# Three of twelve normed tiles transposed by DMA instead of TensorE, their norm weights applied by ScalarE, and a normed-x tile for each batch

## The chip, the core and the metric

The kernel runs on one core of one Trainium2 chip. The metric is the device time of one execution in microseconds (us); less is better. Engines are named as in the profile: PE is TensorE's matmul, PEld its weight load, DVE is VectorE, ACT is ScalarE, POOL is GpSimd, and SP is SyncE, which here only issues DMAs. A trailing q (SPq) means an engine's sequencer.

## What is computed

An attention of the RWKV kind with a decaying state over 4 batches, 8 heads, 768 steps and head size 48, and on its output, as 3072 tokens of width 384, a root-mean-square norm and a gated feed-forward layer of width 1536:

```python
for t in range(S):
    cur = np.einsum('bhd,bhe->bhde', u[None] * kt, vt)
    y[:, :, t] = np.einsum('bhd,bhde->bhe', rt, state + cur)
    state = wt[:, :, :, None] * state + np.einsum('bhd,bhe->bhde', kt, vt)
...
xn = x / np.sqrt(np.mean(x * x, axis=-1, keepdims=True) + 1e-06) * rms_g
g = xn @ w_gate
out = (g / (1 + np.exp(-g)) * (xn @ w_val)) @ w_out
```

Inputs and output are float32. Matmuls run in bf16.

## The kernel before, in words

The sequence is cut into 6 superblocks `n` of 128 steps. A superblock holds 4 batches `j` of 128 tokens each, so 512 tokens. Every piece of work is a step with a name and two numbers, `step.n.j` (or `step.n.f`, where `f` is one of 12 slices of 128 units of the feed-forward layer). One long string, `ORDER`, lists all steps; a loop at the end calls the function of each in turn, and each function issues its instructions at once. So `ORDER` alone sets the order of instructions within each engine, and each engine works in that order; between engines, semaphores make a reader wait for its writer.

For one superblock: `load_*` fetch r, k, v, w (SP). `ln`, `cs_mm`, `cs_add`, `exp_r`, `exp_k`, `r_mul`, `k_mul` make the decayed r and k (ACT, PE, DVE, POOL); `w_tot` makes the state's decay (DVE). `rk_tr` transposes r and k, from superblock 2 on by a DMA that SP issues. `q_mm`, `q_mask_*`, `st_mm`, `st_new`, `y_mm`, `x_add` give the attention's output `xb`, 128 tokens by 384. Then the norm: `x_sq` (ACT) squares and sums, `x_rstd` (POOL) gives the factor, `xn_mul` (ACT) writes the normed `xn` in bf16. The feed-forward layer needs `xn` transposed, with the norm's weights `gT` applied, in the tile `xnt` of 128 x 3 x 512. This is done in two ways:

- superblocks 0 to 3: `xn_pe` makes three 128x128 transposes on PE into PSUM, and `xn_out` (DVE) copies them to `xnt` times `gT`, one instruction of 384 columns;
- superblocks 4 and 5: `xn_tr` transposes by one DMA from SP straight into `xnt`, and `xn_gain` multiplies all 512 tokens by `gT` in place, three instructions a superblock (DVE, one of them ACT).

`gate_mm` and `val_mm` (three matmuls of 512 columns each, line 626) read the whole of `xnt`; `silu` (ACT) and `h_mul` (DVE) give `ht`; `o_mm` (12 matmuls of 384 columns a batch, line 672) and `o_out`, `out_dma` bring the result out. The feed-forward layer of superblock n runs beside the attention of superblock n+1, and `o_mm` of n-1 fills PE between them: while it runs, the transposes for superblock n are made.

PSUM is used in three rings: "a" and "b" with 2 slots each (names `ps_au`, `ps_av`, `ps_bu`, `ps_bv`), taken in turn by `cs_mm`, `cs_add`, `gate_mm` and `val_mm`, and "q" with 4 slots (`ps_qu` and so on) for the rest, the transposes included. A slot goes to the step that asks when its last user is the oldest. `xn` has 3 buffers, taken in `xn_mul`; the squares that `x_sq` has no use for go to one fixed tile, `junk`.

Of the kernel before, what the change touches and what calls it, by code (L numbers as in the profile page):

```python
# [74 lines left out]
exp_k.3.3 cs_mm.3.2 xn_out.2.3 o_mm.1.2 load_r.3.2 k_mul.3.1 w_tot.3.3 rk_tr.3.0 r_mul.3.3 cs_add.3.2 out_dma.1.0
xn_out.2.1 load_v.3.0 exp_r.3.2 gate_mm.2.5 exp_k.3.2 r_mul.3.2 w_tot.3.2 val_mm.2.0 gate_mm.2.0 bonus_mul.3.0
bonus_mul.3.2 k_mul.3.2 o_out.1.3 bonus_sum.3.0 silu.2.5 rk_tr.3.1 load_k.3.3 o_out.1.2 q_mm.3.0 silu.2.0 q_mask_e.3.0
val_mm.2.1 bonus_v.3.0 h_mul.2.0 gate_mm.2.1 load_w.4.1 load_v.3.1 load_k.4.3 st_mm.3.2 k_mul.3.3 q_copy_o.3.0
silu.2.1 rk_tr.3.2 load_v.4.0 rk_tr.3.3 val_mm.2.5 gate_mm.2.11 load_k.4.0 bonus_sum.3.1 cast_v.3.0 out_dma.1.1
load_v.3.3 load_w.5.2 q_mask_e.3.1 q_copy_o.3.1 gate_mm.2.2 silu.2.11 h_mul.2.5 val_mm.2.2 h_mul.2.1 load_w.4.0  # L80
gate_mm.2.3 load_v.4.1 silu.2.2 q_mask_o.3.0 cast_v.3.1 load_r.4.1 bonus_sum.3.2 h_mul.2.2 bonus_v.3.1 gate_mm.2.6
val_mm.2.3 y_mm.3.0 st_new.3.2 st_mm.3.0 silu.2.3 gate_mm.2.4 h_mul.2.3 silu.2.6 q_mask_o.3.1 st_new.3.0 st_mm.3.1
silu.2.4 x_add.3.0 load_k.4.1 gate_mm.2.7 val_mm.2.4 x_sq.3.0 gate_mm.2.10 out_dma.1.2 cast_v.4.0 st_new.3.1
val_mm.2.6 q_mm.3.2 h_mul.2.4 bonus_mul.3.3 h_mul.2.6 silu.2.7 val_mm.2.7 val_mm.2.10 load_w.4.3 x_rstd.3.0 silu.2.10
# [5 lines left out]
o_out.2.0 x_rstd.3.2 xn_mul.3.2 w_tot.4.0 ln.4.2 exp_r.4.1 load_r.5.1 x_rstd.3.3 k_mul.4.0 xn_out.3.0 load_r.4.3  # L90
out_dma.1.3 bonus_sum.4.1 xn_pe.3.1 xn_out.3.1 ln.4.3 exp_k.4.1 bonus_mul.4.2 xn_mul.3.3 r_mul.4.1 k_mul.4.1 w_tot.4.1
out_dma.2.0 o_mm.2.1 cs_mm.4.2 xn_pe.3.3 bonus_mul.4.0 cast_v.4.1 xn_pe.3.2 o_out.2.1 cs_mm.4.3 bonus_sum.4.2
rk_tr.4.0 xn_out.3.3 cs_add.4.3 load_k.5.3 o_mm.2.3 exp_r.4.3 xn_out.3.2 cs_add.4.2 bonus_mul.4.3 r_mul.4.3 w_tot.4.3
exp_k.4.3 exp_r.4.2 rk_tr.4.1 o_out.2.3 exp_k.4.2 load_v.4.2 val_mm.3.1 gate_mm.3.6 bonus_sum.4.0 k_mul.4.3 r_mul.4.2
st_mm.4.0 w_tot.4.2 load_r.5.3 load_k.5.0 val_mm.3.0 o_out.2.2 silu.3.6 st_new.4.0 k_mul.4.2 gate_mm.3.1 q_mm.4.0
cast_v.4.2 out_dma.2.2 bonus_sum.4.3 silu.3.1 gate_mm.3.0 q_copy_o.4.0 silu.3.0 h_mul.3.1 q_copy_o.4.1 gate_mm.3.3
val_mm.3.6 gate_mm.3.8 rk_tr.4.3 q_mask_e.4.0 h_mul.3.0 h_mul.3.6 st_mm.4.1 bonus_v.4.0 q_mask_e.4.1 q_mask_o.4.0
load_r.5.0 bonus_v.4.2 rk_tr.4.2 load_v.5.1 q_mask_o.4.1 bonus_v.4.1 silu.3.3 gate_mm.3.4 val_mm.3.4 val_mm.3.3
y_mm.4.0 silu.3.4 st_new.4.1 gate_mm.3.9 h_mul.3.4 load_v.4.3 load_r.5.2 load_k.5.1 silu.3.8 x_add.4.0 val_mm.3.8
gate_mm.3.2 q_mm.4.2 h_mul.3.3 h_mul.3.8 silu.3.9 val_mm.3.9 load_w.5.1 silu.3.2 gate_mm.3.10 q_mask_e.4.3  # L100
q_copy_o.4.3 y_mm.4.1 h_mul.3.9 bonus_mul.5.3 x_sq.4.0 q_mask_o.4.3 x_rstd.4.0 q_copy_o.4.2 bonus_v.4.3 silu.3.10
x_add.4.1 load_w.5.3 val_mm.3.10 gate_mm.3.7 q_mask_e.4.2 x_sq.4.1 bonus_sum.5.3 xn_mul.4.0 load_w.5.0 x_rstd.4.1
h_mul.3.10 silu.3.7 val_mm.3.2 gate_mm.3.5 h_mul.3.2 load_k.5.2 gate_mm.3.11 q_mask_o.4.2 y_mm.4.2 cast_v.4.3
xn_mul.4.1 val_mm.3.7 silu.3.5 bonus_mul.5.0 x_add.4.2 silu.3.11 ln.5.1 y_mm.4.3 h_mul.3.7 val_mm.3.11 x_add.4.3
load_v.5.3 x_sq.4.2 xn_tr.4.0 h_mul.3.11 x_sq.4.3 xn_tr.4.1 val_mm.3.5 st_mm.4.3 h_mul.3.5 x_rstd.4.2 cs_mm.5.1
cs_add.5.1 ln.5.2 xn_mul.4.2 x_rstd.4.3 o_mm.3.2 o_out.3.2 cs_mm.5.2 xn_tr.4.2 exp_k.5.1 cs_add.5.2 exp_r.5.1 o_mm.3.0
xn_mul.4.3 r_mul.5.1 ln.5.3 ln.5.0 xn_tr.4.3 cs_mm.5.0 st_new.4.3 exp_r.5.2 cast_v.5.3 exp_k.5.2 o_mm.3.1 out_dma.3.2
cs_add.5.0 out_dma.2.3 r_mul.5.2 exp_r.5.0 cs_mm.5.3 r_mul.5.0 st_mm.4.2 exp_k.5.0 cs_add.5.3 exp_r.5.3 o_mm.3.3
bonus_mul.5.1 xn_gain.4.0 xn_gain.4.2 xn_gain.4.1 k_mul.5.0 r_mul.5.3 exp_k.5.3 o_out.3.1 out_dma.2.1 o_out.3.0
# [5 lines left out]
h_mul.4.4 bonus_sum.5.2 q_mm.5.2 q_copy_o.5.2 gate_mm.4.10 val_mm.4.6 bonus_v.5.3 cast_v.5.2 silu.4.8 h_mul.4.5
q_copy_o.5.3 cast_v.5.1 q_mask_e.5.3 q_mask_e.5.2 q_mask_o.5.2 silu.4.10 h_mul.4.6 gate_mm.4.7 x_sq.5.0 y_mm.5.1
q_mask_o.5.3 silu.4.7 bonus_v.5.2 x_rstd.5.0 x_add.5.1 val_mm.4.10 y_mm.5.3 val_mm.4.7 y_mm.5.2 gate_mm.4.11 x_add.5.3
x_sq.5.1 h_mul.4.10 x_sq.5.3 x_rstd.5.1 h_mul.4.7 xn_mul.5.1 val_mm.4.8 out_dma.3.3 gate_mm.4.9 silu.4.11 x_rstd.5.3
xn_mul.5.3 xn_tr.5.1 h_mul.4.8 xn_mul.5.0 val_mm.4.11 xn_tr.5.3 x_add.5.2 x_sq.5.2 x_rstd.5.2 val_mm.4.9 silu.4.9
# [5 lines left out]
val_mm.5.9 gate_mm.5.10 silu.5.9 h_mul.5.6 h_mul.5.9 val_mm.5.8 silu.5.10 val_mm.5.10 gate_mm.5.11 h_mul.5.8
h_mul.5.10 val_mm.5.11 silu.5.11 h_mul.5.11 o_mm.5.0 o_mm.5.3 o_out.5.3 o_mm.5.1 out_dma.5.3 o_out.5.1 o_out.5.0
out_dma.5.0 o_mm.5.2 out_dma.5.1 o_mm.5.4 o_out.5.2 out_dma.5.2 o_out.5.4 out_dma.5.4
# [597 lines left out]
```

## Time and profile before

| | |
|---|---|
| median of 3 runs | 201.12 us (200.55 to 201.53) |
| the profiled execution | 200.28 us, of which the span from first to last instruction is 198.6 us |
| TensorE clock granted | 1.000 of full speed |
| busy share of the span | PE 97%, DVE 76%, ACT 69%, POOL 63% |

The profile is of one execution. Rows of the timeline give start, duration, engine, line, operation, output<-input and, in brackets, the engine's idle time ahead of the row and what ended it; a row with xN joins N like instructions, from the first's start to the last's end. Matmul durations include the time through the pipeline, so the next one starts well before the one before has ended.

### The profile page before, as it was taken

To read this page: it belongs to the slowest core of one execution; us is meant where nothing else is said; L and a number is where in the kernel's file an instruction comes from. 1 tells how busy PE (TensorE), PEld (TensorE's weight loads), DVE (VectorE), ACT (ScalarE), POOL (GpSimd) and SP (SyncE) were. 2 spreads that over 40 slices of the span, in tenths; PEclk is the share of its full clock that TensorE was granted. 3 is DMA by queue.
4 is the path that set the end of the run, shared out by engine and by line. 5 is a ranking of instruction groups with operands and counts; after the bars stand their busy time and mean duration, and the time that the engine had idled before them with its cause. 6 is when DMAs were issued, how large, how long until landed. Compare 5 with 4: busy or idle time off the path is not lost.

```text
span 198.6 us, 4409 instructions
## 1 busy us (share of the span) xinstructions
PE 191.9 (97%) x1577; PEld 113.9 (57%) x1577; DVE 151.4 (76%) x290; ACT 137.3 (69%) x279; POOL 125.2 (63%) x184
## 2 busy tenths in 40 slices
PE   7979998999999999999999999999999999999994
PEld 3556574465665565665556665556655565555562
DVE  6358989989998799987889989987887973173611
ACT  4399989579979569958559959399786683164300
POOL 5378993189399687899939899867686851000000
PEclk9999999999999999999999999999999999999999
DMA  6999999999999998999899879995499012032012
GB/s 153 268 235 176 183 220 203 214 180 211 179 195 224 206 196 196 236 198 207 193 195 225 188 171 204 204 183 107 138 187 208 0 25 60 6 112 83 0 59 101
DMA packets 121566, 32.41 MB, mean 163 GB/s; under 512 B 116420, under 2 KB 120392, under 8 KB 121544
## 3 DMA queue, kind: packets, MB, share of 16 engines
q1 hardware_dynamic: 119504, 28.58, 67.3%
q0 software_dynamic: 2032, 3.54, 10.0%
q8 instruction: 12, 0.20, 0.4%
q14 instruction: 10, 0.08, 0.1%
q10 hardware_dynamic: 8, 0.00, 0.0%
HBM read 25.96 MB, written 4.72 MB: 154 GB/s over the span
## 4 chain that ended last, share of the span: by engine, by line
PE 72%; SPq 18%; DMA 6%; POOL 2%; issue 1%; ACT 0%; POOLq 0%
SPq L248 16%; PE ps_av L626 10%; PE ps_bu L626 10%; PE ps_bv L626 10%; PE ps_au L626 10%; PE ps_qv L672 7%; PE ps_qz L672 7%; PE ps_qu L672 5%; PE ps_qx L672 4%; DMA wo_sb<-in_moe_w_out_dram 4%; DMA vt<-in_v_dram 3%; SPq L261 2%; PE ps_qz L502 1%; PE ps_qx L552 1%; PE ps_av L417 1%
## 5 line engine op out<-in xcount | busy, mean ns | idle before, releaser
L672 PEld LDWEIGHTS <-ht 128*128 128x128 bf16 x300 | 28.2, 98 | 17.0 <-issue 0.5
L626 PEld LDWEIGHTS <-wg_sb 128*128 128x128 bf16 x216 | 23.1, 114 | 19.7 <-DMA wg_sb<-in_moe_w_gate_dram 0.7
L626 PEld LDWEIGHTS <-wv_sb 128*128 128x128 bf16 x216 | 22.8, 114 | 19.0 <-DMA wv_sb<-in_moe_w_val_dram 1.0
L658 DVE TENSOR_TENSOR ht<-ps_bv,sg 128x512 bf16<-128x512 f32 x35 | 24.0, 686 | 10.1 <-PE ps_bv L626 9.2
L235 ACT ACTIVATE sg<-ps_av 128x512 bf16<-128x512 f32 x37 | 22.0, 595 | 12.3 <-PE ps_av L626 12.0
L626 PE MATMUL ps_av<-xnt,wg_sb 128*128 128x512 bf16 x111 | 30.1, 380 | 0.0
L626 PE MATMUL ps_bu<-xnt,wv_sb 128*128 128x512 bf16 x111 | 30.1, 380 | 0.0
L658 DVE TENSOR_TENSOR ht<-ps_bu,sg 128x512 bf16<-128x512 f32 x37 | 25.4, 686 | 6.0 <-PE ps_bu L626 5.2
L626 PE MATMUL ps_bv<-xnt,wv_sb 128*128 128x512 bf16 x105 | 28.5, 380 | 0.6 <-DMA wv_sb<-in_moe_w_val_dram 0.5
L626 PE MATMUL ps_au<-xnt,wg_sb 128*128 128x512 bf16 x105 | 28.5, 380 | 0.2 <-DMA wg_sb<-in_moe_w_gate_dram 0.2
L235 ACT ACTIVATE sg<-ps_au 128x512 bf16<-128x512 f32 x35 | 21.0, 599 | 10.8 <-PE ps_au L626 9.0
L467 POOL TENSOR_TENSOR ruk<-rt,kt 128x384 f32<-128x384 f32 x24 | 24.1, 1003 | 6.6 <-DMA kt<-in_k_dram 4.8
L468 POOL TENSOR_TENSOR ruk<-ruk,u_bc 128x384 f32<-128x384 f32 x24 | 24.4, 1017 | 1.9
L520 POOL TENSOR_SCALAR_AFFINE_SELECT qts<-qts 128x512 bf16<-128x512 bf16 x20 | 12.9, 653 | 15.1 <-ACT qts L513 14.6
L477 POOL TENSOR_TENSOR ydiag<-vt,diag 128x384 f32<-128x384 f32 x24 | 19.9, 833 | 1.0 <-DVE rk L461 0.5
L461 POOL TENSOR_TENSOR rk<-kt,ek 128x384 bf16<-128x384 f32 x16 | 15.9, 1007 | 2.3 <-ACT ek L235 2.3
L672 PE MATMUL ps_qv<-wo_sb,ht 128*128 128x384 bf16 (+1 forms) x96 | 15.0, 306 | 0.0
L672 PE MATMUL ps_qz<-wo_sb,ht 128*128 128x384 bf16 x84 | 14.8, 326 | 0.0
L233 ACT ACT_TABLE_LOAD x10 | 12.8, 1283 | 1.8 <-PEq L709 1.6
L235 ACT ACTIVATE lw<-wt 128x384 bf16<-128x384 f32 (+1 forms) x20 | 11.1, 578 | 4.2 <-DMA wt<-in_w_dram 4.1
L472 DVE TENSOR_REDUCE diag<-ruk 128x8 f32<-128x384 f32 x24 | 12.9, 543 | 0.7 <-POOL ruk L468 0.7
L585 ACT ACTIVATE xn<-xb,rstd 128x384 bf16<-128x384 f32 x20 | 11.8, 605 | 0.8 <-POOL rstd L580 0.8
(180 smaller groups left out, 373.6 us busy)
## 6 DMA issues: line engine op xcount, KB each, us to landing
rt<-in_r_dram SPq DMA_DIRECT2D x24, 192.0 KB, 3.9
kt<-in_k_dram SPq DMA_DIRECT2D x24, 192.0 KB, 4.0
vt<-in_v_dram SPq DMA_DIRECT2D x24, 192.0 KB, 3.7
out_dram<-ob SPq DMA_DIRECT2D x23, 192.0 KB, 2.3
wt<-in_w_dram SPq DMA_DIRECT2D x16, 192.0 KB, 4.0
wt<-in_w_dram SPq DMA_DIRECT2D x4, 384.0 KB, 4.4
wo_sb<-in_moe_w_out_dram POOLq DMA_DIRECT2D x3, 384.0 KB, 7.1
wg_sb<-in_moe_w_gate_dram POOLq DMA_DIRECT2D x1, 768.0 KB, 9.8
```

What stands on the lines that cost most here:

```text
L233: nc.scalar.preload_act_table_set(table_name)
L235: return nc.scalar.activation(**kw).ins
L248: dmas["load_" + which, n, j] = nc.sync.dma_start(out=inp[which, n, j], in_=t[j, :, n * L:(n + 1) * L, :].rearrange("h t d -> t h d")).ins
L461: eng.tensor_tensor(out=rk[:, n % 2, j, 1, :, 0:D], in0=inp["k", n, j], in1=bank["cs_k", n, j][:, 0:DM].rearrange("p (h d) -> p h d", h=H) ...
L467: nc.gpsimd.tensor_tensor(out=ruk[n, j], in0=inp["r", n, j], in1=inp["k", n, j], op=ALU.mult)
L468: nc.gpsimd.tensor_tensor(out=ruk[n, j], in0=ruk[n, j], in1=u_bc, op=ALU.mult)
L472: nc.vector.tensor_reduce(out=diag[n, j].rearrange("p h o -> p (h o)"), in_=ruk[n, j], axis=mybir.AxisListType.X, op=ALU.add)
L477: nc.gpsimd.tensor_tensor(out=ydiag[n, j], in0=inp["v", n, j], in1=diag[n, j].to_broadcast([128, H, D]), op=ALU.mult)
L520: nc.gpsimd.affine_select(out=qts[n, j][:, 1], in_=qts[n, j][:, 1], compare_op=ALU.is_gt, fill=0.0, base=0, pattern=[[0, NP], [1, 128]], c ...
L626: nc.tensor.matmul(ps[:, cols], lhsT=units(ws, c, f), rhs=xnt[n][:, c, cols], start=(first and c == 0), stop=(c == KC - 1))
L658: nc.vector.tensor_tensor(out=ht[n][:, f, :], in0=bank.pop(("v", n, f)), in1=bank.pop(("sg", n, f)), op=ALU.mult)
L672: nc.tensor.matmul(ps[:, cols], lhsT=ht[n][:, f, b * L:(b + 1) * L], rhs=wo_sb[:, f, cols], start=(f == 0), stop=(f == FC - 1))
```

## The change

`ORDER` loses `xn_pe.2.0`, `xn_pe.3.0` and `xn_pe.3.1` and gains `xn_tr.2.0`, `xn_tr.3.0` and `xn_tr.3.1`. For these three, `xn_out` no longer reads PSUM by DVE but multiplies `xnt` in place by ACT, 128 columns in each of three instructions. `xn_out.2.0` moves two steps on, `xn_out.3.0` and `xn_out.3.1` some steps on, and `load_r.3.2` comes earlier, ahead of `xn_tr.2.0`. `xn` now has a buffer for each batch (4), is taken in `x_sq`, and takes the squares too, so that `junk` goes. All else in `ORDER` keeps its sequence; the table is cut here to one line.

```diff
-o_mm.1.3 w_tot.3.1 xn_pe.2.3 o_out.1.1 cs_add.3.3 r_mul.3.1 load_k.3.2 load_r.3.3 xn_pe.2.1 xn_out.2.0 exp_r.3.3
+xn_pe.2.3 o_out.1.1 cs_add.3.3 r_mul.3.1 load_k.3.2 load_r.3.3 load_r.3.2 xn_tr.2.0 xn_pe.2.1 exp_r.3.3 exp_k.3.3
...
     EARLY = 13
+    XT_DMA = sel("30 20 31")
...
-    junk = const.tile([128, DM], BF16)
...
-        nc.scalar.activation(out=junk, in_=xb[n, j], func=AF.Square, accum_out=rstd[n, j][:, 0, c:c + 1])
+        xn = bank["xn", n, j] = pt.tile([128, DM], BF16, name="xn", bufs=SB)
+        nc.scalar.activation(out=xn, in_=xb[n, j], func=AF.Square, accum_out=rstd[n, j][:, 0, c:c + 1])
...
     def xn_mul(n, j):
-        xn = bank["xn", n, j] = pt.tile([128, DM], BF16, name="xn", bufs=3)
+        xn = bank["xn", n, j]
...
             xnt[n] = pt.tile([128, KC, TS], BF16, name="xnt")
+        if (n, j) in XT_DMA:
+            for c in range(KC):
+                t = xnt[n][:, c, j * L:(j + 1) * L]
+                nc.scalar.activation(out=t, in_=t, func=AF.Copy, scale=gT[:, c:c + 1])
+            return
         ps = bank.pop(("xt", n, j))
```

How the instructions stand on SP at the turn to the feed-forward layer of superblock 3. Before (the `rt` are `load_r.4.0` and `load_r.4.2`, then `load_w.4.2`, `load_k.4.2`, `load_r.5.1`, `load_r.4.3`; the `rkT` is `rk_tr.4.0`):

```order
L261 DMA wt<-in_w_dram 128x8x48
L248 DMA rt<-in_r_dram 128x8x48 x2
L261 DMA wt<-in_w_dram 128x8x48
L248 DMA kt<-in_k_dram 128x8x48
L248 DMA rt<-in_r_dram 128x8x48 x2
L687 DMA out_dram<-ob 128x384 x2
L489 DMA_TRANSPOSE rkT<-rk 128x8x128
```

After (lines have moved on by one to six):

```order
L262 DMA wt<-in_w_dram 128x8x48
L249 DMA rt<-in_r_dram 128x8x48
L591 DMA_TRANSPOSE xnt<-xn 128x3x128
L249 DMA rt<-in_r_dram 128x8x48
L262 DMA wt<-in_w_dram 128x8x48
L249 DMA kt<-in_k_dram 128x8x48
L249 DMA rt<-in_r_dram 128x8x48 x2
L693 DMA out_dram<-ob 128x384
L591 DMA_TRANSPOSE xnt<-xn 128x3x128
L693 DMA out_dram<-ob 128x384
L489 DMA_TRANSPOSE rkT<-rk 128x8x128
```

`xn_tr.3.0` has come between the two `rt` loads, so that five loads and an output now stand behind it, and `xn_tr.3.1` between the two outputs.

ACT at the same place, before, from `exp_k.4.1` and `xn_mul.3.3` (line 585) over `o_out.2.1` (681) to `o_out.2.3`:

```order
L235 ACTIVATE ek<-ps_bu 128x384
L585 ACTIVATE xn<-xb,rstd 128x384
L681 COPY ob<-ps_qv 128x384
L235 ACTIVATE ps_av<-ps_av 128x388
L235 ACTIVATE ek<-ps_bv 128x384
L235 ACTIVATE ps_au<-ps_au 128x388
L681 COPY ob<-ps_qv 128x384
```

After:

```order
L236 ACTIVATE ek<-ps_bu 128x384
L586 ACTIVATE xn<-xb,rstd 128x384
L605 ACTIVATE xnt<-xnt,gT 128x128 x3
L687 COPY ob<-ps_qv 128x384
L605 ACTIVATE xnt<-xnt,gT 128x128 x3
L236 ACTIVATE ps_av<-ps_av 128x388
L236 ACTIVATE ek<-ps_bv 128x384
L236 ACTIVATE ps_au<-ps_au 128x388
L687 COPY ob<-ps_qv 128x384
```

The two times three new instructions stand on either side of `o_out.2.1`, both ahead of `exp_r.4.3` (`ps_av`) and `exp_k.4.3` (`ek<-ps_bv`). For superblock 2 the three of `xn_out.2.0` stand between `exp_k.3.3` and `exp_r.3.2`, and `xn_tr.2.0` stands on SP straight ahead of `rk_tr.3.0`.

More of the change, by code (lines that the diff above doesn't have):

```diff
@@ L75 @@
[L75 to L84, printed above, removed]
@@ L90 @@
[L90 to L99, printed above, removed]
@@ L100 @@
[L100 to L109, printed above, removed]
@@ L115 @@
[L115 to L119, printed above, removed]
@@ L125 @@
[L125 to L127 removed]
+load_r.3.0 x_sq.2.2 xn_mul.2.0 cast_v.3.2 cs_add.3.0 x_add.2.3 exp_k.3.0 x_sq.2.3 o_mm.1.0 cs_mm.3.1 exp_r.3.0 ln.3.2
+x_rstd.2.2 o_mm.1.1 st_new.2.3 load_r.3.1 out_dma.0.3 w_tot.3.0 r_mul.3.0 xn_mul.2.1 k_mul.3.0 xn_mul.2.2 cs_add.3.1
@@ new lines @@
+exp_k.3.1 xn_pe.2.2 cs_mm.3.3 x_rstd.2.3 o_out.1.0 exp_r.3.1 bonus_mul.3.1 xn_out.2.2 xn_mul.2.3 o_mm.1.3 w_tot.3.1
+xn_pe.2.3 o_out.1.1 cs_add.3.3 r_mul.3.1 load_k.3.2 load_r.3.3 load_r.3.2 xn_tr.2.0 xn_pe.2.1 exp_r.3.3 exp_k.3.3
+xn_out.2.0 cs_mm.3.2 xn_out.2.3 o_mm.1.2 k_mul.3.1 w_tot.3.3 rk_tr.3.0 r_mul.3.3 cs_add.3.2 out_dma.1.0 xn_out.2.1
+load_v.3.0 exp_r.3.2 gate_mm.2.5 exp_k.3.2 r_mul.3.2 w_tot.3.2 val_mm.2.0 gate_mm.2.0 bonus_mul.3.0 bonus_mul.3.2
+k_mul.3.2 o_out.1.3 bonus_sum.3.0 silu.2.5 rk_tr.3.1 load_k.3.3 o_out.1.2 q_mm.3.0 silu.2.0 q_mask_e.3.0 val_mm.2.1
@@ new lines @@
+x_add.3.3 cs_mm.4.0 bonus_mul.4.1 ln.4.1 cs_mm.4.1 x_sq.3.1 x_add.3.2 x_sq.3.2 cs_add.4.0 h_mul.2.8 st_new.3.3
+o_mm.2.0 x_sq.3.3 o_mm.2.2 exp_r.4.0 load_k.4.2 cs_add.4.1 exp_k.4.0 r_mul.4.0 x_rstd.3.1 xn_mul.3.1 o_out.2.0
+x_rstd.3.2 xn_mul.3.2 w_tot.4.0 ln.4.2 exp_r.4.1 load_r.5.1 x_rstd.3.3 k_mul.4.0 load_r.4.3 out_dma.1.3 xn_tr.3.1
+bonus_sum.4.1 ln.4.3 exp_k.4.1 bonus_mul.4.2 xn_mul.3.3 xn_out.3.0 r_mul.4.1 k_mul.4.1 w_tot.4.1 out_dma.2.0 o_mm.2.1
+cs_mm.4.2 xn_pe.3.3 bonus_mul.4.0 cast_v.4.1 xn_pe.3.2 o_out.2.1 xn_out.3.1 cs_mm.4.3 bonus_sum.4.2 rk_tr.4.0
```

61 lines of the change are left out of this document (44 added, 17 removed).

## The prediction

> **What bounds the kernel now.** I read the page's busy shares first, then the chain that ended last, then the timelines of PE, ACT and SP at the two turns where the three transposes stand.
>
> ```profile
> PE 191.9 (97%) x1577; PEld 113.9 (57%) x1577; DVE 151.4 (76%) x290; ACT 137.3 (69%) x279; POOL 125.2 (63%) x184
> DMA  6999999999999998999899879995499012032012
> PE 72%; SPq 18%; DMA 6%; POOL 2%; issue 1%; ACT 0%; POOLq 0%
> 46.00 7.12 DMA wo_sb<-in_moe_w_out_dram
> 53.16 0.81 PE ps_qx L672 x4
> ...
> 194.63 1.00 PE ps_qv L672 x12
> ```
>
> The chain leaves the loads at 53.16 us and is PE's from there to the end. All that the change moves lies behind that point, in a stretch where PE never waits long: an instruction less on PE is time gained, and a helper's lateness costs only what it makes PE wait. The DMA row matters too: the 16 engines are nearly full until about 130 us, and all three new DMAs fall into that time.
>
> **Off PE: nine transposes.** Three groups go, `xn_pe.2.0`, `xn_pe.3.0` and `xn_pe.3.1`:
>
> ```profile
> 82.66 0.33 PE L596 MATMUL ps_qx<-ident,xn 128*128 128x128 bf16 x3
> 82.83 2.11 PE L672 MATMUL ps_qu<-wo_sb,ht 128*128 128x384 bf16 x12
> 109.32 0.33 PE L596 MATMUL ps_qx<-ident,xn 128*128 128x128 bf16 x3
> 109.48 2.11 PE L672 MATMUL ps_qv<-wo_sb,ht 128*128 128x384 bf16 x12
> 113.38 0.33 PE L596 MATMUL ps_qu<-ident,xn 128*128 128x128 bf16 x3
> 113.55 2.11 PE L672 MATMUL ps_qv<-wo_sb,ht 128*128 128x384 bf16 x12
> ```
>
> A group is shown as 0.33 us, but the next starts 0.17, 0.16 and 0.17 us after it: that is what it takes of PE. The sum is -0.50 us. Nothing else on PE changes but the names of PSUM slots, which I cost at nothing: three users fewer of the "q" ring leave each slot free for longer.
>
> **Off DVE: three copies** of 0.55 us (the last `xn_out` of superblock 2, below, is of that form). DVE is not on the chain, so this is worth nothing by itself.
>
> **Onto ACT: nine instructions of 128 columns.** No row has this size in place. The nearest are one in-place multiply of 512 columns and `xn_mul`, 384 columns:
>
> ```profile
> L612 ACT ACTIVATE xnt<-xnt,gT x1: 712/712/712, 145.0 to 145.0; 128x512 bf16<-128x512 bf16 x1
> L585 ACT ACTIVATE xn<-xb,rstd x20: 597/600/618, 51.5 to 165.4; 128x384 bf16<-128x384 f32 x20
> 111.50 1.10 ACT L585 ACTIVATE xn<-xb,rstd 128x384 bf16<-128x384 f32 x2
> L570 ACT ACTIVATION_READ_ACCUMULATOR junk<-xb 128x1 f32 x20 | 3.8, 189 | 0.0
> ```
>
> The step from 384 to 512 columns is 0.112 us, so 128 columns would be 0.600 - 2 x 0.112 = 0.376 us alone. Two in a row take 1.10 us where 2 x 0.60 would be 1.20, so neighbours overlap by 0.10: three take 0.376 + 2 x 0.276 = 0.93 us. That is my value, as the 512-column row is the same operation on the same tile. The bounds are 3 x 0.189 = 0.57 (the shortest ACT row) and 3 x 0.600 = 1.80.
>
> Where it falls, superblock 2 first, then 3:
>
> ```profile
> 86.73 0.48 ACT L235 ACTIVATE ek<-ps_bu 128x384 f32<-128x384 f32 x1
> 89.19 0.48 ACT L235 ACTIVATE ps_av<-ps_av 128x388 f32<-128x388 f32 x1 [1.97 <-DVE ps_bv L425]
> 89.00 0.55 DVE L607 TENSOR_TENSOR xnt<-ps_qu,gT 128x384 bf16<-128x384 bf16 x1
> 89.70 0.81 PE L626 MATMUL ps_au<-xnt,wg_sb 128*128 128x512 bf16 x3
> 114.11 0.61 ACT L585 ACTIVATE xn<-xb,rstd 128x384 bf16<-128x384 f32 x1
> 115.70 0.48 ACT L681 COPY ob<-ps_qv 128x384 f32<-128x384 f32 x1 [0.99 <-PE ps_qv L672]
> 117.21 0.48 ACT L235 ACTIVATE ps_av<-ps_av 128x388 f32<-128x388 f32 x1 [1.03 <-DVE ps_bv L425]
> 117.60 0.48 ACT L235 ACTIVATE ek<-ps_bv 128x384 f32<-128x384 f32 x1
> 118.31 0.81 PE L626 MATMUL ps_bv<-xnt,wv_sb 128*128 128x512 bf16 x3
> ```
>
> `xn_out.2.0` comes right after the `ek` that ends at 87.21, into 1.97 us in which ACT waits for DVE: 0.93 fits, and even 1.80 does. If that cover were gone, `exp_r.3.2` and PE's first gate matmul at 89.70 would be late, whose other condition, DVE's last `xnt`, ends 0.15 us ahead of it; DVE's queue loses a copy there and can only be earlier.
>
> In superblock 3 ACT idles 0.99 us ahead of `o_out.2.1` and 1.03 ahead of `exp_r.4.3`, 2.02 together, and gets 2 x 0.93 = 1.86. But PE, which ends both waits, is by then 0.50 us earlier, while ACT, dense before, is earlier only by the 0.17 of superblock 2. So 2.02 - 0.33 = 1.69 us are free, and ACT falls 0.17 short. PE's first matmul of superblock 3's layer, at 118.31, needs `ps_bv`, which the `ek` row frees at 118.08: 0.23 us of slack. 0.17 goes into 0.23, so I cost it at nothing. With 0.57 a batch there is 0.55 to spare; with 1.80 ACT is 3.60 - 1.69 = 1.91 late and PE loses 1.91 - 0.23 = 1.68 us. The range for this term is 0 to +1.68.
>
> **Onto SP and the DMA engines: three transposes.**
>
> ```profile
> L590 SPq DMA_TRANSPOSE xnt<-xn x8: 1178/1198/1390, 133.5 to 166.0; - x8
> DMA to landing us min/median/max: 2.3/2.3/3.1
> DMA to landing us min/median/max: 2.7/3.3/3.8
> q1 hardware_dynamic: 1258, 0.30, 29.4%
> 80.84 2.00 SPq L248 DMA_DIRECT2D rt<-in_r_dram  x2
> 83.90 1.36 SPq L489 DMA_TRANSPOSE rkT<-rk  x1
> 104.19 0.78 SPq L248 DMA_DIRECT2D rt<-in_r_dram  x1
> 105.58 0.61 ACT L585 ACTIVATE xn<-xb,rstd 128x384 bf16<-128x384 f32 x1
> 106.60 0.70 SPq L261 DMA_DIRECT2D wt<-in_w_dram  x1
> 110.17 3.18 SPq L687 DMA_DIRECT2D out_dram<-ob  x2
> SPq L687 <- DVE wcol L451: 1.9, 1, 1.9
> 113.46 1.34 SPq L489 DMA_TRANSPOSE rkT<-rk  x1
> 112.50 0.51 ACT L235 ACTIVATE lw<-wt 128x384 bf16<-128x384 f32 x1
> wt<-in_w_dram SPq DMA_DIRECT2D x1, 192.0 KB, 3.6
> ```
>
> The first landing row is of `xn`'s transposes, in a time of little traffic; the second of `rk`'s, in the full time; the 29.4% is of a window of 4.5 us with three `xn` transposes, 0.44 us of all 16 engines for each.
>
> `xn_tr.2.0` is free to go when the two `rt` issues end at 82.84. It takes 1.2 us of SP and lands at 82.84 + 2.3 to 3.8, at the latest 86.6, before ACT gets to it (87.21, or 0.17 earlier). `rk_tr.3.0` behind it moves from 83.90 to some 84.05: nothing.
>
> `xn_tr.3.0` must wait for `xn_mul.3.0`, which ends at 106.19; without it SP would issue the second `rt` when the first ends, at 104.97. With the issue of 1.2 us, all behind it (the loads `load_r.4.2`, `load_w.4.2`, `load_k.4.2`, `load_r.5.1`, `load_r.4.3` and `out_dma.1.3`) is issued up to 2.3 us later. What hides this is the 1.9 us that SP then spends waiting at `out_dma.2.0`, and that the loads land when the full DMA engines get to them, not when they are issued: DMA's own loss is the 0.44 us and whatever the pause leaves idle. I take 0.5 to 1 us. The first in need is `ln.4.2` (the `lw` row at 112.50), whose `wt` was issued at 106.60; a landing of 3.6 us (the last row, of the window with this load alone) gives 110.2 and 2.3 us of slack.
>
> `xn_tr.3.1` needs `xn_mul.3.1`, the first of the pair at 111.50, ended at 112.1. I take it issued at 112.7, for SP has caught up most of its delay, and landed 2.7 later (the least of `rk`'s row, as DMA thins out there), 115.4. ACT wants it after `o_out.2.1`, at about 115.85. So it lands in time, by 0.4 us. `out_dma.2.0` and `rk_tr.4.0` behind it start some 0.3 to 0.6 later; `rk_tr.4.1`, which the pair in `q_mm.4.0` needs last, waits for POOL anyway. Bounds: 0, and as in the second rival below.
>
> Squares into `xn`: the same instruction with another target, nothing. Four buffers in place of three: `x_sq` waits for the reader of one superblock ago, long done.
>
> **Sum.** -0.50 + 0 + 0 = -0.50 us: the profiled execution would be 200.28 - 0.50 = 199.78 us, a span of 198.1. It was 0.84 us below the median of the runs, so on their scale 201.12 - 0.50 = 200.6 us. That is 0.25%; I count under 0.5%, 1.0 us, as no change, about what a measurement of this kernel can tell.
>
> **Rivals.**
>
> *ACT's instructions overlap less.* With 0.376 each and no overlap, 1.13 a batch, ACT falls 2.26 - 1.69 = 0.57 short, PE waits 0.34 and the time is 201.0 us. For it: in-place instructions of one tile might each wait for the end of the one before. Against: they write different columns, and the overlap is in every joined ACT row. The Trainium skill (ScalarE: Activation LUTs, Rules for kernel authors) budgets about 0.3 us for an ACTIVATE and 0.83 ns an element, an estimate of 0.41 us each and 1.22 us a batch. By that rule PE would wait some 0.5 us and nothing would be gained; the trace's 0.712 us for 512 columns agrees with it (0.3 + 0.42 = 0.72), but its joined rows are shorter than the rule's sum.
>
> *The transpose lands late and stops ACT (slower).* If SP does not catch up, `out_dma.1.3` (in the row of two outputs, 110.17 + 3.18 less the wait of 1.9 and the second's 0.4, at 111.1) ends at 113.4, and `xn_tr.3.1` lands 3.8 later, at 117.2. `xn_out.3.1` then ends at 118.1, against 116.7 when `exp_r.4.3` could start: 1.4 late, less 0.23 of slack, PE loses 1.2, net +0.7, 201.8 us. If it queues behind loads as `wt` did earlier (4.9 us), it lands at 118.3 and the net is +1.8, 202.9 us:
>
> ```profile
> wt<-in_w_dram SPq DMA_DIRECT2D x3, 192.0 KB, 4.9
> ```
>
> It costs from a landing at 116.1 on, outweighs the gain from 116.6, and is slower by 1.0 us from 117.6. For it: DMA is full up to 110. Against: SP's 1.9 us wait, and thin traffic after 112.
>
> *The transposes were worth their full duration.* Each is 0.217 us in the rows (0.33 for three, overlapped); nine unoverlapped are 1.95 us, 199.2 us. Against it stand the starts 0.17 us on. The Trainium skill (TensorE: Matmul & The Clock Gate, Part 4: PE-mode transpose) gives about 275 ns for one in a kernel; nine would be an estimate of 2.5 us and 198.6. The trace disagrees: here the same transpose holds PE for 55 ns.
>
> **How the numbers follow.** Gain kept whole or nearly (200.2 to 200.9): 0.55, since all three covers are found in rows, though one by only 0.06 us. Eaten in part or up to +0.7 by ACT's overlap or a landing up to 117.2 (200.9 to 201.9): 0.27. Late beyond that: 0.12. Full duration or another gain that I don't see: 0.06. The likeliest gives 200.6. The range 200.0 to 201.9 leaves out 0.06 and 0.12. Faster by over 0.5% gets 0.10 (the last case and an edge of the first, as the runs themselves differ by 1 us), slower 0.12, no change 0.78.
>
> **What would show it.** Right: PE's groups at line 626 start 0.17 us earlier after superblock 2's turn and 0.5 after 3's; the three ACT groups (`xnt<-xnt,gT` 128x128) spaced under 0.3 us with no long wait for DMA ahead; landings of `xn_tr.3.1` before ACT reaches it. Wrong: idle time of ACT ended by DMA `xnt<-xn`, or a gap on PE at 117 to 119 or before `silu.3.6`; or `ln.4.2` waiting for its `wt`.

## The result, and the profile after

The changed kernel is slower: 201.75 us (median of 22 executions, 200.86 to 203.87) where the kernel before, run beside it, has 200.67 (22, 199.52 to 202.03). The ratio is 1.0067, 95% interval 1.0044 to 1.0090; a second measurement (below) gives 1.0049 [1.0022, 1.0077]. The forecast was 200.6 us, "no change", with a range up to 201.9. The profiled execution has 201.74 us and a span of 200.0. Its granted clock is 0.997, but the trace has it at full speed up to 198.8 us, after PE's last matmul, so the clock explains nothing here. One profiled execution, that of e10 below, ran at a granted clock of 0.854 and took 222.68 us; its profile is not used.

The busy shares and the DMA row of the page after, and the share of the chain that ended last by line (cut to that row):

```profile
PE 191.8 (96%) x1568; PEld 113.3 (57%) x1568; DVE 150.3 (75%) x287; ACT 139.8 (70%) x288; POOL 125.2 (63%) x184
DMA  6999999989989999989988959996499002022012
PE ps_av L632 12%; PE ps_bu L632 11%; PE ps_au L632 11%; PE ps_bv L632 11%; PE ps_qx L678 6%; DMA wg_sb<-in_moe_w_gate_dram 5%; PE ps_qv L678 5%; PE ps_qz L678 5%; SPq L249 5%; PE ps_qu L678 4%; DMA rt<-in_r_dram 2%; SPq L262 2%; DMA xnt<-xn 2%; DMA kt<-in_k_dram 2%; PE ps_qz L502 1%
```

Nine matmuls are gone from PE and 2.5 us have come onto ACT. New on the chain is `DMA xnt<-xn`, 2%. The chain in order of time between 110 and 120 us (start, duration, what) names the place:

```profile
109.35 3.58 DMA kt<-in_k_dram
112.93 0.32 ACT lw L236
113.25 4.20 DMA xnt<-xn
117.45 0.02 issue
117.48 0.96 ACT xnt L605 x3
118.44 0.34 issue
118.78 0.48 ACT ek L236
119.26 0.04 issue
119.30 0.81 PE ps_bv L632 x3
```

`xn_tr.3.1` is 4.20 us under way from the start of its issue; ACT multiplies the moment it has landed, frees `ps_bv` by `ek`, and only then can PE begin superblock 3's layer. The timelines of ACT and PE show the waits:

```profile
87.72 0.98 ACT L605 ACTIVATE xnt<-xnt,gT 128x128 bf16<-128x128 bf16 x3
115.02 0.98 ACT L605 ACTIVATE xnt<-xnt,gT 128x128 bf16<-128x128 bf16 x3
117.48 0.98 ACT L605 ACTIVATE xnt<-xnt,gT 128x128 bf16<-128x128 bf16 x3 [1.02 <-DMA xnt<-xn]
116.64 2.11 PE L678 MATMUL ps_qv<-wo_sb,ht 128*128 128x384 bf16 x12
119.30 0.81 PE L632 MATMUL ps_bv<-xnt,wv_sb 128*128 128x512 bf16 x3 [0.55 <-ACT ek L236]
```

The last two rows start 2.66 us apart; before it was 1.95 (from the row below to 118.31). PE loses 0.71 us there.

```profile
116.36 2.11 PE L672 MATMUL ps_qv<-wo_sb,ht 128*128 128x384 bf16 x12
```

That is one of two losses. For the other, four starts on PE and the span's end, from the PE timelines (all us):

| | first `o_mm` of superblock 1's layer | first matmul of layer 3 | of layer 4 | of layer 5 | span's end | "way": layer 4 less `o_mm` | "end": span less layer 5 |
|---|---|---|---|---|---|---|---|
| before | 80.45 | 118.31 | 145.87 | 172.09 | 198.57 | 65.42 | 26.48 |
| after | 81.23 | 119.30 | 146.85 | 173.07 | 200.02 | 65.62 | 26.95 |

The first column is read from these rows, of before and of after:

```profile
80.45 2.11 PE L672 MATMUL ps_qz<-wo_sb,ht 128*128 128x384 bf16 x12
81.23 2.11 PE L678 MATMUL ps_qz<-wo_sb,ht 128*128 128x384 bf16 x12
```

The difference of 1.46 us between the two executions is +0.78 ahead of the first moved transpose (the kernels' instructions are alike up to there but for buffers), -0.50 of transposes, +0.71 at superblock 3, and the rest, +0.47, at the end, where nothing was moved. These two measures, way and end, serve for all experiments, since the start differs between executions by up to 1.4 us (80.0 to 81.4 in 18 profiles, among them 79.99 and 81.12 for kernels with no transpose moved). It follows that a time in one profile is comparable with a time in another only after the difference of the two starts is taken off.

### The profile page after: what moved, and what is told of

The parts are those of the page before. It is cut to its first block, busy times and chain, and to the rows that moved or that the text cites. A ratio compares the mean times of both kernels' runs of the same rounds, so it can differ in the third digit from the quotient of the medians.

```text
span 200.0 us, 4401 instructions
## 1 busy us (share of the span) xinstructions
PE 191.8 (96%) x1568; PEld 113.3 (57%) x1568; DVE 150.3 (75%) x287; ACT 139.8 (70%) x288; POOL 125.2 (63%) x184
## 4 chain that ended last, share of the span: by engine, by line
PE 74%; DMA 11%; SPq 7%; POOL 3%; issue 2%; ACT 1%; POOLq 0%
PE ps_av L632 12%; PE ps_bu L632 11%; PE ps_au L632 11%; PE ps_bv L632 11%; PE ps_qx L678 6%; DMA wg_sb<-in_moe_w_gate_dram 5%; PE ps_qv L678 5%; PE ps_qz L678 5%; SPq L249 5%; PE ps_qu L678 4%; DMA rt<-in_r_dram 2%; SPq L262 2%; DMA xnt<-xn 2%; DMA kt<-in_k_dram 2%; PE ps_qz L502 1%
## 5 line engine op out<-in xcount | busy, mean ns | idle before, releaser
L678 PE MATMUL ps_qx<-wo_sb,ht 128*128 128x384 bf16 x84 | 14.9, 325 | 0.0
L678 PE MATMUL ps_qz<-wo_sb,ht 128*128 128x384 bf16 x72 | 12.7, 326 | 0.0
```

Source lines behind the costliest of these rows:

```text
L678: nc.tensor.matmul(ps[:, cols], lhsT=ht[n][:, f, b * L:(b + 1) * L], rhs=wo_sb[:, f, cols], start=(f == 0), stop=(f == FC - 1))
```

## The experiments

Each was timed against the kernel before on the same chip, in 5 rounds of alternating executions (12 executions of each experiment), unless it says otherwise.

**e1: the buffers alone.** The order of before, with the tiles of the change (cut to the main lines):

```diff
-        nc.scalar.activation(out=junk, in_=xb[n, j], func=AF.Square, accum_out=rstd[n, j][:, 0, c:c + 1])
+        xn = bank["xn", n, j] = pt.tile([128, DM], BF16, name="xn", bufs=SB)
+        nc.scalar.activation(out=xn, in_=xb[n, j], func=AF.Square, accum_out=rstd[n, j][:, 0, c:c + 1])
```

> Only the buffer part: the squares of x_sq go into xn, xn has 4 buffers, junk is gone; all twelve early tiles are transposed by PE as in the kernel before. Theory T (the turn at superblock 3): the loss of the change comes from the stop of ACT at xn_out.3.1, so this run is as the kernel before, 200.7 us, ratio 1.000 within 0.003, and PE reaches the o_mm group behind xn_pe.2.0 at about 82.8 us as in the profile before. Rival B (buffers): the change's profile was 0.78 us late already ahead of its first transpose, so the buffers and the shifted tiles make the start slower; then this run is 0.8 to 1.1 us slower, 201.5 to 201.8, and that group starts at 83.4 or later. Rival C (chance): the start varies from execution to execution by this much in any kernel.

Measured 200.11 us, ratio 0.9977 [0.9953, 1.0000]; start 79.99, way 65.42, end 26.5. The buffers cost nothing, and the later start of the changed kernel's profile does not come from them. In this profile nothing is gained either, so a ratio of 0.998 is about what a measurement here gives for no difference.

**e3, e4: fewer transposes moved.** e3 puts batch 1 of superblock 3 back on PE, e4 moves that of superblock 2 alone.

```diff
-    XT_DMA = sel("30 20 31")
+    XT_DMA = sel("30 20")        # e3; e4: sel("20"), and ORDER accordingly
```

> The change with batch 1 of superblock 3 back on PE and DVE, two transposes left by DMA (2.0 and 3.0). Theory T: no stop of ACT for a late transpose is left, PE saves 6 x 0.055 = 0.33 us and loses nothing, 200.7 - 0.33 = 200.35 us; no wait of PE for ACT ahead of the first matmul of superblock 3's layer. Rival B (buffers): 0.8 us more than that, 201.2. Rival D (a transpose by DMA costs wherever it is put, by the delay of loads and other transposes behind it on SP): 201.3 or more, two thirds of the change's loss.

> Only batch 0 of superblock 2 by DMA, its weights by ACT, with the change's buffers; superblock 3 wholly on PE. Theory T: saves 3 x 0.055 = 0.17 us, 200.5 us. Rival B (buffers): 201.3 to 201.6. Rival D: a third of the change's loss, 201.0.

e3: 200.55 us, 0.9986 [0.9967, 1.0005]; way 65.08. e4: 200.83, 0.9992 [0.9966, 1.0018]; way 65.25. So each tile (three transposes) that PE is spared shortens the way by 0.17 us, as forecast, as long as `xn_tr.3.1` is not among them. The times alone show no difference from before. The ends: e3 26.9, e4 26.5.

**e5: the late multiply moved back.** All three by DMA, `xn_out.3.1` behind `exp_k.4.3` on ACT.

```diff
-xn_pe.3.2 o_out.2.1 xn_out.3.1 cs_mm.4.3
+xn_pe.3.2 o_out.2.1 cs_mm.4.3
...
-w_tot.4.3 exp_k.4.3 exp_r.4.2
+w_tot.4.3 exp_k.4.3 xn_out.3.1 exp_r.4.2
```

> The change whole, but xn_out.3.1 stands on ACT behind exp_r.4.3 and exp_k.4.3 instead of ahead of them, so that the wait for the transpose no longer holds up the two exponentials that free PSUM for PE. Theory T: the transpose lands at 117.5 as in the change's profile, PE now waits for xnt itself, until about 118.5, 0.2 to 0.3 us, in place of the 0.55 us for ACT: 0.3 us faster than the change, 201.4 by its median, and the row ahead of PE's first matmul of superblock 3's layer names ACT xnt, not ACT ek. If the transpose lands by 116.6 the whole wait goes: 201.0. Rivals B and D: no difference from the change, 201.75.

Measured 201.10 us, 1.0001 [0.9981, 1.0021]; way 65.32, end 27.0, and 2.06 us instead of 2.66 from `o_mm.2.3` to layer 3. The transpose landed at 117.5 as late as in the changed kernel, but ACT no longer stood in front of `exp_r.4.3` while it waited. PE now waits for `xnt` itself, in the first groups of the layer: three matmuls take 0.96 us instead of 0.81.

```profile
118.46 0.96 PE L632 MATMUL ps_bv<-xnt,wv_sb 128*128 128x512 bf16 x3
```

From the layer's first matmul to layer 4 it is 27.85 us instead of 27.56, so that 0.29 us of the gain is lost again. The wait for the transpose is the loss, and ACT's place in it makes it larger; that ACT's work by itself costs nothing is seen in e13, where the multiplies stand in their first place and the transpose lands in time.

**e6, e7: the end.** SP's DMAs signal eight semaphores ("lanes") in turn, and at the program's end SP waits for each lane, one after the other. Three more DMAs move the last output from lane 6 to lane 1. e6 adds five tiny loads to the changed kernel (lane 6 again), e7 three to the kernel before (lane 1):

```diff
+    def lane(n, j):
+        nc.sync.dma_start(out=spare[0:1, 4 * j:4 * j + 4], in_=moe_rms_g.rearrange("(c p) -> c p", p=128)[0:1, 0:4])
...
-xn_tr.5.2 xn_gain.5.1
+xn_tr.5.2 lane.0.0 lane.0.1 lane.0.2 xn_gain.5.1
```

> The changed kernel with five tiny loads (16 bytes each) on SP behind xn_tr.5.2, so that the last output's DMA sits again on the semaphore lane (6) that it has in the kernel before, instead of lane 1. Theory (lanes: SP waits for the lanes one after the other at the end, and those behind the last output's lane are waited for after it has landed): from the first gate matmul of superblock 5's layer to the span's end 26.9 us becomes 26.5, the time falls by 0.4 us against the changed kernel, and the stall of PE ahead of superblock 3's layer (0.55 to 0.70 us) stays. Rival (the longer end is chance of the execution, or comes from the order of the outputs): 26.9 us stays.

> The kernel before with three tiny loads on SP behind xn_tr.5.2, so that its last output's DMA sits on lane 1, as in the changed kernel; no transpose is moved. Theory (lanes): the end grows from 26.5 to 26.9 us, the time by 0.4 us (ratio 1.002), and nothing else differs. Rival (the end depends on what the change moved): 26.5 us and a ratio of 1.000.

e6: end 26.5, way 65.51, 201.16 us, 1.0029 [1.0004, 1.0054]. e7: end 26.9, 201.14 us, 1.0023 [1.0002, 1.0043], way 65.42 as before. e7 costs 0.46 us without moving a transpose. SP's own waits at the end, of before, after and e7 (engine line, what it waited for: us in total, times, longest):

```profile
SPq L720 <- DMA out_dram<-ob: 0.5, 1, 0.5
```

```profile
SPq L726 <- DMA out_dram<-ob: 1.3, 2, 0.8
```

```profile
SPq L723 <- DMA out_dram<-ob: 1.3, 2, 0.7
```

In all 18 profiles used, the end is 26.5 us where the last DMA has lane 6 or 7 (nine runs) and 26.9 to 27.1 where it has lane 0 or 1 (nine). That the place of the last DMA sets the end is shown. With lane 1, the waits for lanes 2 to 7 come after the landing, one every 0.06 us; with lane 6, only the one for lane 7. From landing to the span's end it is 0.97 us in before and 1.28 in after and in e7, 0.31 of the 0.47. The other 0.16 is the last output itself, which lands 1.74 us after its issue in after (1.73 in e7) and 1.59 in before; why is open.

**e8, e9: why `xn_tr.3.1` lands late.** The trace records the landing of a DMA as 16 steps of its semaphore, here called its parts. In the changed kernel 15 of the transpose's 16 parts are done at 115.94 and the last at 117.45. Between 114.89 and 116.37 one of the 16 DMA engines carries a 16 KB fetch of PE's instructions (one packet of queue q8). In e8 five warm-up matmuls at the start are cut in pieces, nine instructions more with the same columns, so that the fetch should move; in e9 the transpose goes ahead of an output:

```diff
-        nc.tensor.matmul(psum("q", None, [128, DM]), lhsT=still, rhs=bc_mid(still, KC), start=True, stop=True)
+        ps = psum("q", None, [128, DM])
+        for a, b in ((0, 1), (1, 2), (2, 3)) if i < 4 else ((0, 1), (1, 3)) if i == 4 else ((0, 3),):
+            nc.tensor.matmul(ps[:, a * 128:b * 128], lhsT=still, rhs=bc_mid(still, b - a), start=True, stop=True)
```

```diff
-load_r.4.3 out_dma.1.3 xn_tr.3.1 bonus_sum.4.1
+load_r.4.3 xn_tr.3.1 out_dma.1.3 bonus_sum.4.1
```

> The changed kernel with five of the 13 warm-up matmuls at the start cut into pieces of 128 or 256 columns, the same columns in all but nine matmuls more, so that PE's instruction stream is as long ahead of superblock 3's layer as before. Theory (the landing of xn_tr.3.1 was delayed because one sixteenth of it stood behind a 16 KB fetch of PE's instructions, which comes at fixed places of that stream): the fetch near 114.9 us moves back to about 112.3, xn_tr.3.1 lands 2.6 to 2.8 us after its issue instead of 4.2, the wait of xn_out.3.1 of 1.02 us and the stall of 0.55 us ahead of superblock 3's layer go (to 0.15 or less), and the time falls by 0.5 us against the changed kernel; the end stays at 26.9. Rival (the landing is late because xn_tr.3.0 blocks SP, so that xn_tr.3.1 is issued late, or since two transposes are in flight): 4.2 us from issue to landing and the stall stay.

> The changed kernel with xn_tr.3.1 ahead of out_dma.1.3 on SP instead of behind it. Theory (issue and fetch): the issue begins when xn_mul.3.1 is done, some 0.8 us earlier, most of its parts land 0.8 us earlier, ahead of the fetch at 114.9 us, so it lands by about 115.1 and the stall ahead of superblock 3's layer goes (0.15 or less): 0.5 us less than the changed kernel. Rival (the transpose takes 4.2 us from issue to landing in this place whatever else runs): it lands at about 116.6, ACT still waits some 0.2 us and the stall falls only to about 0.2. Rival two (rk_tr.4.0 or out_dma.1.3, now later, become the wait): a stall on DVE or on q_mm instead.

Neither removed the stall in its profile. e8: 201.58 us, 1.0049 [1.0015, 1.0082], way 65.70. e9: a way of 66.02 in its profile, of an execution of 201.38 us; its times, 200.76 and 1.0008 [0.9984, 1.0033], lie below the changed kernel's, so that this profile may not stand for the rest. SP's and PE's rows of e8, then of e9 with its landing:

```profile
112.58 1.92 SPq L695 DMA_DIRECT2D out_dram<-ob  x1
114.60 1.18 SPq L593 DMA_TRANSPOSE xnt<-xn  x1
119.12 0.81 PE L634 MATMUL ps_bv<-xnt,wv_sb 128*128 128x512 bf16 x2 [0.63 <-ACT ek L236]
```

```profile
112.28 1.41 SPq L591 DMA_TRANSPOSE xnt<-xn  x1
118.93 0.81 PE L632 MATMUL ps_bv<-xnt,wv_sb 128*128 128x512 bf16 x2 [0.94 <-ACT ek L236]
DMA to landing us min/median/max: 4.8/4.8/4.8
```

In e8 the fetch came at 113.08, at the time of the two loads ahead: their last parts came at 115.61 and 116.26, 1.1 to 1.6 us after the others, and SP's next issues took longer (1.92 us for `out_dma.1.3`, which took 1.18 in after), so that the transpose was issued only at 114.60 and landed at 117.27. That the edit moved the fetch is not shown: in e6, whose PE instructions are those of the changed kernel, it came at 113.70 and the same two loads were late in the same way (last parts at 115.91 and 116.50, the transpose at 117.47). In e9 the transpose was issued 1 us earlier, had 15 parts done at 115.51 and the 16th at 117.08, with a fetch from 115.08. So neither a moved fetch nor a place ahead of the output is enough: the transpose stands in a full queue, and it is late where a fetch falls on it or on what is ahead of it.

**e10, e13, e14, e15: less ahead of it.** As e9, and `load_r.5.1` too, which superblock 5 needs, goes behind the transpose; with the five tiny loads.

```diff
-w_tot.4.0 ln.4.2 exp_r.4.1 load_r.5.1 x_rstd.3.3 k_mul.4.0 load_r.4.3 out_dma.1.3 xn_tr.3.1 bonus_sum.4.1
+w_tot.4.0 ln.4.2 exp_r.4.1 x_rstd.3.3 k_mul.4.0 load_r.4.3 xn_tr.3.1 out_dma.1.3 bonus_sum.4.1
...
-out_dma.2.0 o_mm.2.1
+out_dma.2.0 load_r.5.1 o_mm.2.1
```

> The changed kernel with load_r.5.1 (read a superblock later) and out_dma.1.3 behind xn_tr.3.1 on SP, so that nothing but load_r.4.3 stands ahead of it, and with the five tiny loads that put the last output on lane 6. Theory (the DMA engines are full there: xn_tr.3.1 lands when what SP issued ahead of it has drained, and one engine is held another 1 to 1.5 us by the instruction fetch that falls there in every execution): with two transfers of 192 KB less ahead of it, it lands at about 115.1, or by 116.5 where the fetch meets it; the stall of 0.4 to 0.9 us ahead of superblock 3's layer goes (0.15 or less), the way from o_mm.1.0 to superblock 4's layer is 65.0 to 65.1 us (65.42 before), the end is 26.5, and the time is some 0.4 us below the kernel before (ratio 0.998). Rival (the transpose itself needs over 4 us in this place): it lands at 117 again, the stall stays, and the time is that of the five tiny loads alone, some 0.4 us above before.

> The same kernel as e10_less_ahead once more, for a profile at full clock: e10's time (ratio 1.001) is above what the theory gave it (0.998). If the full DMA engines made the landing late: xn_tr.3.1 lands by 116.5 us at the latest, no stall of PE over 0.15 us ahead of superblock 3's layer, the way from o_mm.1.0 to superblock 4's layer 65.0 to 65.1 us and the end 26.5 us. If the transpose needs over 4 us in this place whatever stands ahead of it: landing at 117, stall 0.4 us or more. If the stall has only moved (load_r.5.1 or out_dma.1.3 late): no stall there, but one of 0.3 us or more behind it.

e10: 200.68 us, 1.0010 [0.9985, 1.0035]. e13, the same kernel: 200.84, 1.0021 [0.9992, 1.0050], profiled at 199.88. The 0.998 expected did not come: neither is told from before. e13's transpose, landing and PE:

```profile
111.49 1.19 SPq L591 DMA_TRANSPOSE xnt<-xn  x1
DMA to landing us min/median/max: 2.4/2.4/2.4
117.55 0.81 PE L632 MATMUL ps_bv<-xnt,wv_sb 128*128 128x512 bf16 x3
120.97 0.23 PE L502 MATMUL ps_qz<-rkT 48*128 48x128 bf16 x1 [0.17 <-DMA rkT<-rk]
```

It lands 2.4 us after its issue, at 113.9, the fetch (113.84) falls on the outputs behind it, and PE's stall at superblock 3 is gone. But the way is 65.25 and not 64.92, before less the 0.50 of three tiles: PE now waits at `q_mm.4.1` for `rk_tr.4.1`. Whether that varies was asked with one more profile each (single executions):

> The kernel of e13_less_ahead2, another execution. If what the fetch meets decides: xn_tr.3.1 lands by 114 us where the fetch comes behind it, up to 1.5 us later where it meets it; no stall over 0.15 us ahead of superblock 3's layer either way, but where it meets rk_tr.4.0 or the loads behind, PE waits 0.3 us or more at q_mm.4. If the slower executions are slow elsewhere: the way from o_mm.1.0 to superblock 4's layer is 65.2 to 65.3 us again and the time differs by the start.

> As e14_less_ahead, another execution: the way is 65.2 to 65.3 us, or longer by a wait at q_mm.4.

200.18 and 201.17 us; landings 114.1 and 115.0, no stall over 0.07 us ahead of layer 3, and at `q_mm.4.1`, of e14 and of e15:

```profile
121.27 0.23 PE L502 MATMUL ps_qz<-rkT 48*128 48x128 bf16 x1 [0.37 <-DVE diag L472]
```

```profile
122.27 0.23 PE L502 MATMUL ps_qz<-rkT 48*128 48x128 bf16 x1 [0.62 <-DMA rkT<-rk]
```

The ways are 65.51 and 65.71: the time won at superblock 3 was given back 3 us later, differently in each execution.

**e11: without the late transpose.** e3 with six tiny loads (`lane.0.0` to `lane.0.5`, lane 6).

> xn_tr.2.0 and xn_tr.3.0 by DMA, batch 1 of superblock 3 on PE, and six tiny loads that put the last output on lane 6. Theory: the way from o_mm.1.0 to superblock 4's layer 65.08 us as without the tiny loads, the end 26.5 instead of 26.9 us; the time 0.4 us below the same without them, 200.1 us where before has 200.7 (ratio 0.9965). Rival (the end's 0.4 us is given back elsewhere): ratio 0.9986 as without them.

200.26 us, 0.9981 [0.9961, 1.0001]; way 65.14, end 26.5. Both terms are as expected in the profile; the ratio's interval holds both theories' figures, so the times don't tell them apart.

**e12, e16, e17: the changed kernel again,** e12 timed, the others single executions.

> The changed kernel once more, beside the other two. If the stall ahead of superblock 3's layer belongs to the change and not to the one execution that was profiled: a stall of 0.4 to 0.7 us again, xn_tr.3.1 landing over 3.5 us after its issue began, the end 26.9 us, ratio 1.003 to 1.007. If it was chance: no stall, and a ratio of 1.002 from the end alone.

> The changed kernel, another execution. The stall ahead of superblock 3's layer is 0.4 to 0.9 us, the way from o_mm.1.0 to superblock 4's layer 65.5 to 66.0 us, the end 26.9 us. If the executions spread for another reason, the difference between executions lies ahead of o_mm.1.0 (80 to 81.4 us in the runs so far, whatever the kernel).

> As e16_after, another execution: stall 0.4 to 0.9 us, way 65.5 to 66.0 us, end 26.9 us.

e12: 201.44 us, 1.0049 [1.0022, 1.0077]; e16 and e17: 201.78 and 201.79. PE at superblock 3, of the three in turn:

```profile
118.53 0.81 PE L632 MATMUL ps_bv<-xnt,wv_sb 128*128 128x512 bf16 x3 [0.66 <-ACT ek L236]
```

```profile
119.33 0.81 PE L632 MATMUL ps_bv<-xnt,wv_sb 128*128 128x512 bf16 x3 [0.92 <-ACT ek L236]
```

```profile
119.25 0.81 PE L632 MATMUL ps_bv<-xnt,wv_sb 128*128 128x512 bf16 x3 [0.53 <-ACT ek L236]
```

Four profiles of this program of four have the stall, and in all four 15 parts of `xn_tr.3.1` land 2.7 to 3.2 us after its issue (which is at 113.25, 112.36, 112.74 and 113.17) and the 16th 1.5 us after them, with a fetch begun at 114.5 to 115.3. The ways are 65.62, 65.73, 65.99 and 65.61, on average 0.32 us over before, the ends 0.5 to 0.6 over.

**e18: both loads later.** As e13, with `load_r.5.1` and `load_k.5.3` behind `rk_tr.4.1` and `load_v.4.2`.

```diff
-rk_tr.4.1 o_out.2.3 exp_k.4.2 load_v.4.2 val_mm.3.1
+rk_tr.4.1 o_out.2.3 exp_k.4.2 load_v.4.2 load_r.5.1 load_k.5.3 val_mm.3.1
```

> As e13_less_ahead2 with load_r.5.1 and load_k.5.3 behind rk_tr.4.1 and load_v.4.2. Theory (the wait at q_mm.4.1 came from those two loads): xn_tr.3.1 lands by 114.2 to 115.1 us, rk_tr.4.1 begins by 116.5, PE waits nowhere over 0.15 us in superblock 3's layer, the way from o_mm.1.0 to superblock 4's layer is 64.9 to 65.1 us (before 65.42), the end 26.5, ratio 0.998 (0.996 to 1.000). Rival (something else in these executions is slow): the way is 65.2 us or more, or the way is short and the ratio still 1.001 or more.

200.12 us, ratio 0.9973 [0.9946, 0.9999]: the one version with all three transposes moved whose interval lies below 1, if barely, and e1 has much the same ratio without any gain. The end is 26.5. In its profile nothing waits at superblock 3 or at `q_mm.4.1`, but the way is 65.25, not the 64.9 to 65.1 expected, for one transpose of r and k is late further on:

```profile
128.69 0.23 PE L502 MATMUL ps_qx<-rkT 48*128 48x128 bf16 x1 [0.27 <-DMA rkT<-rk]
```

The fetch came at 112.33 here, earlier than in e13 to e15 (113.8 to 114.6), and made no part late. So this one profile does not tell whether the moved loads or the earlier fetch took the wait at `q_mm.4.1` away.

## Why the prediction was wrong

*PE's transposes, -0.50: right.* e3 and e4 show 0.17 us for each group of three. The "full duration" rival falls, and with it the estimate of 2.5 us from the Trainium skill (TensorE: Matmul & The Clock Gate, Part 4).

*ACT's nine instructions: right in price and in cover.* One takes 0.39 us (0.376 forecast), three 0.98 (0.93):

```profile
L605 ACT ACTIVATE xnt<-xnt,gT x9: 385/393/402, 87.7 to 118.1; 128x128 bf16<-128x128 bf16 x9
```

The Trainium skill's rule (ScalarE: Activation LUTs, Rules for kernel authors) gives an estimate of 0.41 us for one, near the row; three times that, 1.22, is not what joined rows show. At superblock 3 the cover held too: in e13, with the transpose in time, PE's layer starts without a stall. Superblock 2 went as forecast; the issue of `xn_tr.2.0` took 1.82 us instead of 1.2, at no cost.

*The landing of `xn_tr.3.1`, 115.4: this step failed, by the 2.7 us from issue to landing.* 115.4 was 112.7 + 2.7, on the clock of the profile before. The changed profile starts 0.78 us later (81.23 against 80.45), so its issue at 113.25 stands at 112.47 on that clock: not late, but 0.23 us early. In e12, e16 and e17 the same reckoning gives 112.46, 112.30 and 112.43. What took longer is the rest: 15 of 16 parts were down 2.69 us after the issue, at 115.94, but the transpose is done only with the last, at 117.45, 4.20 us after it (4.2 to 4.8 in the four profiles). On the clock of before that is 116.67, so it is 1.27 us late, and the 16th part's 1.51 us is more than all of it. In e13 to e15, where the fetch fell on what stands behind the transpose, it landed 2.4 to 2.7 us after its issue.

The time of the issue was right for a wrong reason, which is luck. I let SP catch up "in the 1.9 us that SP then spends waiting at `out_dma.2.0`". That wait lies *behind* `xn_tr.3.1` in SP's queue; it could help `rk_tr.4.0`, not the transpose. SP caught up by shorter issues: on the clock of before, the load right behind `xn_tr.3.0` (108.10 below) is 2.35 us late, but its issue took 0.58 us instead of some 1.6; the load after it (108.72) is 1.34 late and `out_dma.1.3` (111.97) 1.02. SP's rows after:

```profile
105.35 0.91 SPq L249 DMA_DIRECT2D rt<-in_r_dram  x1
106.83 1.22 SPq L591 DMA_TRANSPOSE xnt<-xn  x1
108.10 0.58 SPq L249 DMA_DIRECT2D rt<-in_r_dram  x1
108.72 0.58 SPq L262 DMA_DIRECT2D wt<-in_w_dram  x1
...
110.28 1.65 SPq L249 DMA_DIRECT2D rt<-in_r_dram  x2
111.97 1.18 SPq L693 DMA_DIRECT2D out_dram<-ob  x1
113.25 1.20 SPq L591 DMA_TRANSPOSE xnt<-xn  x1
114.55 0.52 SPq L693 DMA_DIRECT2D out_dram<-ob  x1
115.17 2.31 SPq L489 DMA_TRANSPOSE rkT<-rk  x1
```

I also counted on traffic to thin out after 112. The DMA busy share in 40 slices of 0.1 us from 112 to 116, of before and of after:

```profile
DMA  9999853110000000103899962002999999999800
```

```profile
DMA  9999999999999999999999985899942110038799
```

In before the engines run empty from 112.5 on, for more than a microsecond. In after the loads held up by `xn_tr.3.0` keep them full to 114.9 (114.1 on the clock of before), so the thin stretch that I read belonged to the old order of issues, although 15 parts kept to the 2.7 without it. The 16th came behind them with the instruction fetch of 114.89 to 116.37; that the fetch held it rests on coincidence in time (last section). The old trace had the like: a fetch from 112.31 on, and `out_dma.1.3` with 15 parts by 113.27 and one at 115.00. It was an output that nobody waited for, and I did not look at single parts.

*The rival "the transpose lands late and stops ACT"* gave 117.2, PE losing 1.2 and 201.8 us, with 0.27 for landings up to there. Its ending came, by another way: it let SP not catch up, but the issue was in time. On the clock of before the landing was 116.67, past the 116.1 from which the prediction counts a cost. PE lost 0.71, for ACT reached `exp_r.4.3` only 0.9 us later than in e5 (1.73 us after the start of `o_mm.2.3`, there 0.85), and there was slack. That its total agrees with the measured 201.75 is luck, as the end added 0.47.

*`rk_tr.4.1` was put at nothing*, since it "waits for POOL anyway". The stall hid that: with the stall gone, PE waits for it in e13 and e15, and their ways are 0.33 and 0.79 us above 64.92.

*The end of the program stood in no term of the sum.* Three more DMAs on SP were costed where they stand, not by where they leave the last one in the turn of semaphores. That is 0.46 us in e7 and 0.47 to 0.59 in the four profiles of the changed kernel, about as much as the transposes won.

The two shown losses and the gain make +0.32 (way, mean of four profiles) and +0.51 (end, of the same), 0.83 us or 0.4%. That lies within the second measurement (0.2 to 0.8%); the first (0.4 to 0.9%) leaves up to 1.0 us that no run accounts for. Executions of the changed kernel spread more than those of before (standard deviation 0.9 and 0.8 us, before 0.67 and 0.54). The ways of its four profiles differ by 0.4 us at most, too little to make that; its cause is open.

## What to carry to other kernels

A transfer is done when its last sixteenth is. Here a transfer on the critical path needed a margin of about 1.5 us over the landing of its other parts, or less work ahead of it in its queue (e13 to e15, e18), while a load that is needed late can go behind. Before work is moved onto a queue, read which instructions stand ahead of the wait that is to absorb it, and what the new wait does to the traffic that was thin in the old trace. Compare two traces from a start that they share: what looked like an issue 0.55 us late was an execution that began 0.78 us later. And look where a program's last DMA falls among the semaphores: 0.4 us of the end could be had by five loads of 16 bytes.
